# ScalarE's queue in place of SyncE's for the loads of q, k and v in an attention and mixture-of-experts kernel

## The chip, the cores and the metric

The kernel runs on one core of a Trainium2 chip. The metric is the time of one execution in device microseconds. Before the change it is 1074.55 us, the median of 3 runs (1073.31 to 1079.6).

## The reference

There are two parts, one after the other. The first is attention over 8 batches of 8 heads, 576 positions and a head size of 64, in which scores more than tau below the row's maximum are thrown away:

```python
scores = scale * np.matmul(q, k.transpose(0, 1, 3, 2))
thresh = np.max(scores, axis=-1, keepdims=True) - tau
scores = np.where(scores >= thresh, scores, -1000000000.0)
attn = np.exp(scores - np.max(scores, axis=-1, keepdims=True))
attn = attn / (np.sum(attn, axis=-1, keepdims=True) + 1e-09)
return np.matmul(attn, v)
```

The second part takes the 4608 rows of 512 numbers that come out, sends each row to one of 8 experts (the largest of 8 gate logits), computes `relu(x @ w1[e]) @ w2[e]` with 1024 hidden units and multiplies by the gate's probability.

## The kernel before

Each float32 operand is kept as a float16 pair, a high part and a low part (the rest), and a product is made of three float16 matmuls. The names end in `h`/`l` or `hi`/`lo` for these parts.

Attention goes by pairs of heads: 32 pairs, numbered n, one head in the lower 64 partitions and one in the upper. The program is written as one long list of steps, 11 per pair. A step k does one unit of scores (`s_unit`, for the row's maximum, TensorE L294 and L296, VectorE L306) of a pair that lies 21 steps ahead, one unit of transposed scores (`st_unit`, TensorE L342 and L343) of the present pair, the exponential of it on ScalarE (L359), the mask on VectorE (L362), the split of the result into two float16 parts (ScalarE's cast L367, GpSimd's subtraction L368), and a piece of the product with v (`av_piece`, L400 to L409). Beside these, functions are planned to certain steps with `plan` and `after`.

What a pair needs beforehand is done in three planned functions:

- `load_qk(n)` (L191) brings q and k of a pair, 128 partitions of 1152 float32, 576 KB, into the tile `qkf`. There are two such buffers, so the load of pair n has to wait until VectorE has made the low part of pair n-2. It is planned 15 steps ahead of `stack(n)`.
- `split(n)` (L201) makes the high part on ScalarE (L212, `hi<-qkf`, which waits for the load), and the low part in three pieces on TensorE (L226) and VectorE (L227).
- `stack(n)` (L229) copies both parts, by 12 small DMAs on SyncE's queue and one of constants, to where the matmuls read them (`QK`, `ck`, `CQ`). Later `rows` (L328) adds three rows of thresholds to `CQ` (L330).

`load_v(g)` (L196) brings v of two pairs, 640 KB, into `vf`, of which there is one buffer; `split_v` (L254) splits it with two instructions on ScalarE (L258, `vop<-vf`) and four on VectorE (L227).

When a batch is finished, its rows are normalized, written in the order of the experts to a table in device memory (`xs`), transposed by DMA on SyncE's queue (L469) and routed. The experts' matmuls (L792, L819) fill the time from about 690 us on; their weights `wf` are loaded on SyncE's queue (L697) from 512 KB pieces.

All DMAs but the indirect ones (GpSimd) are issued by SyncE. A scheduler takes the list of steps and sorts each engine's instructions by a model of its own, so that an instruction can stand earlier or later in its engine's queue than it was written; the queue of an engine then runs strictly in that order. DMAs of SyncE and ScalarE take turns in eight completion semaphores, and a DMA also waits until the one eight places before it has landed.

Of the kernel before, what the change touches and what calls it, by code (L numbers as in the profile page):

```python
# [50 lines left out]
def kernel(  # L51
# [9 lines left out]
    nc = tc.nc  # L61
# [128 lines left out]

    def load_qk(n):  # L191
        qkf = ld.tile([P, 2, S], F32, tag="qkf", name=f"qkf_{n}")
        nc.sync.dma_start(qkf, qk[n])
        st[n] = dict(qkf=qkf, Ph={}, Pl={})

    def load_v(g):  # L196
        vf = op.tile([P, 2, 10, D], F32, tag="vf", name=f"vf_{g}", bufs=1)
        nc.sync.dma_start(vf, v[g])
        gr[g] = dict(vf=vf)

    def split(n, lag=1):  # L201
# [666 lines left out]
    for n in range(NPAIR):  # L868

        k = NSTEP * (n - 1) - LEAD - SL  # L870
        if n >= 2:
            plan(max(first, k - LL), lambda n=n: load_qk(n))
        if n:
            plan(max(first, k - TUNE["sp0"]), lambda n=n: split(n))
            plan(max(first + 2, k), lambda n=n: stack(n))
    for g in range(NG):
        k = 2 * NSTEP * g
        plan(k + TUNE["sv0"], lambda g=g: split_v(g, 0))
        plan(k + TUNE["sv1"], lambda g=g: split_v(g, 1))
        if g:  # L880
            plan(k + TUNE["lv"], lambda g=g: load_v(g))
# [146 lines left out]

    if True:
        load_qk(0)  # L1030
        load_qk(1)
        load_v(0)
        split(0, 0)
        stack(0)
# [4 lines left out]
        while busy:  # L1039
# [3 lines left out]
            for z in (("st", "s"), ("s", "st"))[TUNE["ord"]]:  # L1043
                n, t = divmod(k + (NSTEP + LEAD if z == "s" else 0), NSTEP)
# [11 lines left out]
            n, t = divmod(k - TUNE["av"], NSTEP)  # L1056
# [94 lines left out]
```

## Time and profile before

| | |
|---|---|
| time, median of 3 runs | 1074.55 us (1073.31 to 1079.6) |
| time of the profiled execution | 1082.59 us |
| its span, from the first to the last instruction | 1080.9 us |
| granted TensorE clock, mean | 0.963 |
| loads of q and k, of v | 32 of 576 KB, 16 of 640 KB |

The profiled execution is one of the slower ones, 0.7% over the median. The profile gives for each engine the time in which it worked; DMA issues and waits are not counted as work. A transfer runs beside all engines, so what it costs can only be seen where an engine stands idle before the instruction that reads it. The rows of the section on the trace are from this execution.

### The profile page before, as it was taken

How to read it: one execution, taken by the hardware profiler on the slowest of the kernel's cores; microseconds unless marked ns; L12 is line 12 of the kernel's file. 1: busy time of each engine (PE TensorE's matmuls, PEld its weight loads, DVE VectorE, ACT ScalarE, POOL GpSimd, SP SyncE). 2: the span in 40 equal slices, each digit the busy share in tenths (PEclk: the TensorE clock that was granted, in tenths of full speed). 3: DMA queues.
4: the chain of work that ended last, by engine and by line, in shares of the span. 5: the costliest groups of instructions: out<-in, count | busy, mean ns of one | idle time of the engine just before them, and what ended most of it. 6: DMA issues, size and time to landing. Idle time of an engine off the chain costs nothing.

```text
span 1080.9 us, 27283 instructions
## 1 busy us (share of the span) xinstructions
PE 967.8 (90%) x10856; PEld 622.8 (58%) x10856; DVE 725.9 (67%) x1443; ACT 651.0 (60%) x1066; POOL 560.4 (52%) x460
## 2 busy tenths in 40 slices
PE   4889999799898998898897689678999999999996
PEld 1355555455555565464564366556767667766783
DVE  7888999788887989897899966451623324324550
ACT  2588887887878877787777664322433423424641
POOL 3265967876786957968667674134221222211221
PEclk9999999999999999998997789899999999999999
DMA  6435554654464643735634339869946557557620
GB/s 191 129 81 128 126 131 110 142 117 123 124 153 122 129 123 100 179 92 157 141 75 145 96 90 254 218 220 177 256 151 216 148 164 217 156 154 219 211 99 24
DMA packets 142557, 159.09 MB, mean 147 GB/s; under 512 B 96345, under 2 KB 112731, under 8 KB 142428
## 3 DMA queue, kind: packets, MB, share of 16 engines
q1 hardware_dynamic: 133276, 127.88, 46.2%
q0 software_dynamic: 9152, 29.45, 8.7%
q8 instruction: 86, 1.41, 0.5%
q14 instruction: 43, 0.35, 0.1%
HBM read 90.24 MB, written 19.44 MB: 101 GB/s over the span
## 4 chain that ended last, share of the span: by engine, by line
PE 56%; DMA 12%; DVE 7%; ACT 5%; POOL 5%; issue 4%; SPq 1%; POOLq 0%; DVEq 0%; ACTq 0%
PE h L792 18%; PE y L819 16%; PE st L342 4%; PE s L294 3%; PE st L343 3%; PE s L296 3%; DVE e L362 3%; POOL pl L368 2%; PE av L408 2%; ACT e L359 2%; ACT ph L367 2%; PE av L407 2%; PE av L409 2%; DVE nm L306 2%; DMA qkf<-in_qk_dram 2%
## 5 line engine op out<-in xcount | busy, mean ns | idle before, releaser
L368 POOL TENSOR_TENSOR pl<-e,ph 128x1024 f16<-128x1024 f32 x158 | 335.2, 2133 | 160.9 <-ACT ph L367 117.3
L362 DVE SCALAR_TENSOR_TENSOR e<-st,e 128x512 f32<-128x512 f32 (+1 forms) x352 | 221.4, 637 | 45.6 <-ACT e L359 42.9
L359 ACT ACTIVATE e<-st,ntau 128x512 f32<-128x512 f32 (+1 forms) x352 | 222.9, 650 | 37.6 <-PE st L343 34.7
L306 DVE TENSOR_REDUCE nm<-s 128x1 f32<-128x512 f32 x320 | 200.3, 632 | 33.4 <-PE s L296 32.4
L792 PEld LDWEIGHTS <-wb 128*128 128x128 f16 x2304 | 193.5, 100 | 30.4 <-DMA xTm<-R 8.4
L792 PE MATMUL h<-xTm,wb 128*128 128x256 f16 (+2 forms) x2112 | 199.0, 256 | 9.5 <-DMA xTm<-R 9.5
L819 PE MATMUL y<-wb,hl 128*128 128x512 f16 (+1 forms) x1056 | 201.3, 360 | 0.0
L367 ACT CAST ph<-e 128x1024 f16<-128x1024 f32 x160 | 166.3, 1041 | 14.5 <-DVE e L362 14.2
L408 PE MATMUL av<-vop,pl 128*128 128x65 f16 (+1 forms) x1280 | 163.2, 196 | 6.5 <-POOL pl L368 6.3
L294 PE MATMUL s<-QK 128*128 128x512 f16 (+3 forms) x640 | 141.7, 298 | 29.0 <-DMA QK<-lo 16.0
L407 PE MATMUL av<-vop,ph 128*128 128x64 f16 (+1 forms) x1280 | 164.1, 196 | 1.3 <-ACT ph L367 1.3
L409 PE MATMUL av<-vop,ph 128*128 128x65 f16 (+1 forms) x1280 | 163.1, 196 | 0.0
L711 DVE SCALAR_TENSOR_TENSOR wb<-wf,wb 128x1024 f16<-128x1024 f32 x96 | 129.4, 1384 | 49.8 <-ACT wb L710 48.5
L342 PE MATMUL st<-QK 128*128 128x512 f16 (+3 forms) x640 | 142.2, 299 | 17.2 <-DVE e L362 12.0
L819 PEld LDWEIGHTS <-hl 128*128 128x128 f16 (+1 forms) x1056 | 94.2, 100 | 98.5 <-issue 1.9
L343 PE MATMUL st<-CQ,ck 128*128 128x512 f16 (+3 forms) x640 | 141.0, 296 | 6.1 <-DMA CQ<-ptT 5.1
L408 PEld LDWEIGHTS <-pl 128*128 128x128 f16 (+1 forms) x1280 | 122.3, 102 | 41.7 <-POOL pl L368 17.7
L296 PE MATMUL s<-ck,CQ 128*128 128x512 f16 (+3 forms) x640 | 140.3, 294 | 0.0
L407 PEld LDWEIGHTS <-ph 128*128 128x128 f16 (+1 forms) x1280 | 123.3, 102 | 19.9 <-issue 8.0
L409 PEld LDWEIGHTS <-ph 128*128 128x128 f16 (+1 forms) x1280 | 122.3, 101 | 18.7 <-issue 8.6
L710 ACT ACTIVATE wb<-wf 128x1024 f16<-128x1024 f32 x96 | 97.5, 1050 | 41.1 <-DMA wf<-in_w_dram 23.0
L780 ACT ACTIVATE hl<-h 128x512 f16<-128x512 f32 (+1 forms) x80 | 45.6, 572 | 123.7 <-PE h L792 121.7
(189 smaller groups left out, 1151.1 us busy)
## 6 DMA issues: line engine op xcount, KB each, us to landing
wf<-in_w_dram SPq DMA_DIRECT2D x96, 512.0 KB
qkf<-in_qk_dram SPq DMA_DIRECT2D x32, 576.0 KB
vf<-in_v_dram SPq DMA_DIRECT2D x16, 640.0 KB
QK<-hi SPq DMA_DIRECT2D x64, 144.0 KB
QK<-hi SPq DMA_DIRECT2D x64, 72.0 KB
QK<-lo SPq DMA_DIRECT2D x64, 72.0 KB
ck<-lo SPq DMA_DIRECT2D x64, 72.0 KB
CQ<-hi SPq DMA_DIRECT2D x64, 64.0 KB
```

Of the source, the lines that this page charges most:

```text
L294: nc.tensor.matmul(sc[rows, oc], d["QA"][a][:, cols], d["KB"][a][:, CH[c]], start=True, stop=False)
L306: nc.vector.tensor_reduce(o, sc[:, 0:width(t)], axis=AX.X, op=ALU.max, negate=True)
L342: nc.tensor.matmul(sc[rows, oc], d["KB"][a][:, cols], d["QA"][a][:, CH[c]], start=True, stop=False)
L359: nc.scalar.activation(pf, sc, AF.Exp, bias=ntau, scale=0.125 / SS)
L362: nc.vector.scalar_tensor_tensor(pf, sc, 0.0, pf, ALU.is_ge, ALU.mult)
L367: nc.scalar.copy(h, pd)
L368: (nc.vector if (n, t) in PLV else nc.gpsimd).tensor_tensor(l, pd, h, ALU.subtract)
L407: nc.tensor.matmul(av[rows, a, 0:D], h, vop[:, tv, W:W + D], start=False, stop=False)
L408: nc.tensor.matmul(av[rows, a], l, vop[:, tv, 0:W], start=False, stop=False)
L409: nc.tensor.matmul(av[rows, a], h, vop[:, tv, 0:W], start=False, stop=a == 1 and i >= 2 and j == NT - 1)
L792: nc.tensor.matmul(o, Wt[:, c, wh, f], x, start=c == 0 and z == 0, stop=c == 3 and z == 2,)
L819: nc.tensor.matmul(o, h[:, hh], Wt[:, f, wh, c], start=f == 0 and z == 0, stop=f == 7 and z == 2)
```

## The change

The loads of pair 2 and later pairs of heads, and those of v from the second group of two pairs on, are issued by ScalarE. These are 30 of the 32 loads of q and k and 15 of the 16 of v. Everything else stays with the engine that has it.

```diff
     def load_qk(n):
         qkf = ld.tile([P, 2, S], F32, tag="qkf", name=f"qkf_{n}")
-        nc.sync.dma_start(qkf, qk[n])
+        (nc.sync if n < 2 else nc.scalar).dma_start(qkf, qk[n])
         st[n] = dict(qkf=qkf, Ph={}, Pl={})
 
     def load_v(g):
         vf = op.tile([P, 2, 10, D], F32, tag="vf", name=f"vf_{g}", bufs=1)
-        nc.sync.dma_start(vf, v[g])
+        (nc.sync if g == 0 else nc.scalar).dma_start(vf, v[g])
         gr[g] = dict(vf=vf)
```

The scheduler sorts again, so the queues differ in more than the moved lines. SyncE's queue before, at the loads for v of group 3 and for q and k of pair 9 (about 116 to 124 us in the trace before); `qkf_2057` is q and k of pair 9, `vf_1911` is v of group 3:

```order
L246 DMA ck_0_159<-lo_1728 64x576
L330 DMA CQ_162<-ptT_1734 1x9x128
L246 DMA ck_1_160<-lo_1728 64x576
L198 DMA vf_1911<-in_v_dram 128x1280
L193 DMA qkf_2057<-in_qk_dram 128x1152
L243 DMA QK_0_2181<-hi_2085 64x1152
L245 DMA QK_0_2181<-hi_2085 64x576
L251 DMA CQ_161<-hi_2085 64x512
```

And the same place of SyncE's queue now:

```order
L330 DMA CQ_162<-ptT_1734 1x9x128
L246 DMA ck_0_159<-lo_1728 64x576
L246 DMA ck_1_160<-lo_1728 64x576
L243 DMA QK_0_2181<-hi_2085 64x1152
L245 DMA QK_0_2181<-hi_2085 64x576
L251 DMA CQ_161<-hi_2085 64x512
```

The two loads are gone from between the copies of pair 7 into `ck` and those of pair 8 into `QK`, and the row of thresholds stands one place earlier. ScalarE's queue now, from the cast before the load to the split that reads it (`hi_2453<-qkf_2057`):

```order
L367 CAST ph_2_1739<-e_2_1738 128x1024
L193 DMA qkf_2057<-in_qk_dram 128x1152
L359 ACTIVATE e_8_1817<-st_8_1812,ntau 128x512
L198 DMA vf_1911<-in_v_dram 128x1280
L359 ACTIVATE e_10_1861<-st_10_1856,ntau 128x64
L417 COPY x_907<-av_0_1756 128x3x130
L359 ACTIVATE e_8_1817<-st_9_1888,ntau 128x512
L419 COPY x_907<-av_3_1872 128x130
L420 COPY xh_906<-av_3_1872 64x130
L367 CAST phc_10_1862<-e_10_1861 128x64
L359 ACTIVATE e_4_1928<-st_4_1925,ntau 128x512
L212 ACTIVATE hi_2453<-qkf_2057 128x1152
```

Nine rows stand between the load of q and k and the split that reads it. ScalarE's queue before, at the same place, from the row that follows the loads' time to the two splits (the split of v is `vop_166<-vf_1911`):

```order
L359 ACTIVATE e_4_1928<-st_4_1925,ntau 128x512
L367 CAST phc_10_1862<-e_10_1861 128x64
L359 ACTIVATE e_4_1928<-st_5_1951,ntau 128x512
L461 CAST R<-xn_0_2143 128x4x128
L367 CAST ph_8_1818<-e_8_1817 128x1024
L258 ACTIVATE vop_166<-vf_1911 128x10x64 x2
L359 ACTIVATE e_6_1978<-st_6_1975,ntau 128x512
L461 CAST R<-xn_1_2298 128x4x128
L359 ACTIVATE e_6_1978<-st_7_2001,ntau 128x512
L212 ACTIVATE hi_2453<-qkf_2057 128x1152
```

Before, the split of v stood ahead of that of q and k; now the split of q and k comes first, and that of v five rows behind it.

## Rows read from the trace of the kernel before

**Rows 1.** Busy times by stage: the window, its length, busy us of each engine (xinstructions), clock, DMA.

```profile
40.00:540.00 500.00, 457.57 (x6158) 273.17 (x6157) 425.77 (x898) 403.39 (x703) 370.60 (x237) 0.98 0.52 127
690.00:1081.00 391.00, 371.44 (x3009) 262.64 (x3006) 152.41 (x247) 146.06 (x193) 90.55 (x116) 0.98 0.60 172
```

**Rows 2.** ScalarE's groups by line and shape, 40 to 540 us: busy, mean ns, idle before, releasers.

```profile
L359 ACT ACTIVATE e<-st,ntau 128x512 f32<-128x512 f32 x270 | 179.9, 684 | 18.9 <-PE st L343 17.0 <-issue 0.3 <-POOL pl L368 0.3
L212 ACT ACTIVATE hi<-qkf 128x1152 f16<-128x1152 f32 x28 | 32.5, 1162 | 23.1 <-DMA qkf<-in_qk_dram 11.2 <-DMA QK<-hi 8.5 <-DMA CQ<-hi 2.4
L258 ACT ACTIVATE vop<-vf 128x640 f16<-128x640 f32 x28 | 20.2, 741 | 20.8 <-DMA vf<-in_v_dram 20.8
L417 ACT COPY x<-av 128x390 f32<-128x390 f32 x26 | 12.5, 481 | 11.7 <-PE av L409 10.3 <-PE av L408 1.4
L359 ACT ACTIVATE e<-st,ntau 128x64 f32<-128x64 f32 x27 | 8.4, 310 | 2.2 <-PE st L343 1.8
```

**Rows 3.** SyncE's issues in order of time: start us, length us, line, operation, transfer.

```profile
99.06 0.45 SPq L193 DMA_DIRECT2D qkf<-in_qk_dram  x1
...
116.65 0.48 SPq L246 DMA_DIRECT2D ck<-lo  x1
117.22 0.54 SPq L198 DMA_DIRECT2D vf<-in_v_dram  x1
117.81 0.44 SPq L193 DMA_DIRECT2D qkf<-in_qk_dram  x1
```

**Rows 4.** ScalarE in order of time: start us, length us, line, operation, [idle before, releaser].

```profile
99.34 0.23 ACT L367 CAST phc<-e 128x64 f16<-128x64 f32 x1
99.47 0.27 ACT L419 COPY x<-av 128x130 f32<-128x130 f32 x1
...
104.99 1.16 ACT L212 ACTIVATE hi<-qkf 128x1152 f16<-128x1152 f32 x1 [1.77 <-DMA CQ<-hi]
...
113.85 1.05 ACT L367 CAST ph<-e 128x1024 f16<-128x1024 f32 x1
...
121.41 1.37 ACT L258 ACTIVATE vop<-vf 128x640 f16<-128x640 f32 x2 [0.69 <-DMA vf<-in_v_dram]
```

**Rows 5.** VectorE in order of time, the last reads of the two loaded buffers.

```profile
113.67 0.53 DVE L227 SCALAR_TENSOR_TENSOR lo<-qkf,hi 128x384 f16<-128x384 f32 x1
...
114.73 0.47 DVE L227 SCALAR_TENSOR_TENSOR vop<-vf,hi_v 128x320 f16<-128x320 f32 x1
```

**Rows 6.** Lines of DMA issues, 40 to 540 us: count, shortest/median/longest ns, first and last.

```profile
L193 SPq DMA_DIRECT2D qkf<-in_qk_dram x27: 414/448/1222, 48.9 to 529.1; - x27
L198 SPq DMA_DIRECT2D vf<-in_v_dram x14: 389/535/587, 48.3 to 528.6; - x14
L469 SPq DMA_TRANSPOSE xTg<-R x27: 1254/1267/2237, 125.0 to 529.7; - x27
L549 POOL DMA_INDIRECT xs<-R,posi x22: 983/1007/1194, 194.0 to 505.5; - x22
```

**Rows 7.** Who waited for whom, 40 to 540 us: us in total, times, longest us.

```profile
PE av L400 <- ACT ph L367: 6.2, 6, 2.6
PE s L294 <- DVE e L362: 5.8, 6, 2.8
PE av L408 <- POOL pl L368: 4.6, 11, 0.7
PE av L401 <- POOL pl L368: 4.3, 7, 1.4
PE st L342 <- DVE e L362: 4.2, 9, 1.2
...
PE st L343 <- DMA CQ<-ptT: 1.2, 2, 0.6
...
DVE e L362 <- ACT e L359: 38.2, 45, 4.3
```

**Rows 8.** The chain that ended last, 40 to 540 us: start us, length us, what.

```profile
206.16 6.26 DMA qkf<-in_qk_dram
```

## The prediction

> **What bounds the kernel now.** I read the stages first, then ScalarE's groups in the stage that the change touches, then single loads, then what TensorE waits for. The change moves only loads of q, k and v, and all but four of its 45 loads fall between 40 and 540 us. In that stage [rows 1] the busy times are 458 us on TensorE, 426 on VectorE, 403 on ScalarE and 371 on GpSimd out of 500. Nothing is saturated: each pair of heads (18.5 us, 27 pairs in 500 us) goes round through all four. From 690 us on TensorE is busy 371 us of 391 with the experts' matmuls, no load of q, k or v is left there, and the change cannot reach it.
>
> The reader should look at what ScalarE waits for [rows 2]. It is idle 500 − 403 = 97 us in the stage, and 23.1 us of that stand before the split of q and k (L212), 20.8 before the split of v (L258), together 43.9 us, all put down to DMAs. Part of L212's is put down to QK<-hi and CQ<-hi, but those transfers read a buffer that is two pairs old, and the program's order issues them long before the new load. At 104.99 the split starts after 1.77 us of idleness "for CQ<-hi" [rows 4]; SyncE had issued that pair's load only at 99.06 [rows 3], 5.93 us earlier. So I count all 43.9 us as late loads.
>
> Why are they late? At 117.22 and 117.81 SyncE issues v and then q and k [rows 3]. VectorE had done with the buffer of q and k at 113.67 + 0.53 = 114.20, and with that of v at 114.73 + 0.47 = 115.20 [rows 5]. SyncE was not waiting for them: it was issuing small copies, the last from 116.65 to 117.13 [rows 3]. The queue's order made these loads 2.0 us and 3.6 us late.
>
> **The change part by part.** *SyncE* loses 30 issues of 0.448 us and 15 of 0.535 [rows 6], 13.4 + 8.0 = 21.5 us. What stands behind them in its queue, the copies into QK, ck and CQ and the rows of thresholds, goes out sooner. TensorE's only listed wait for such a transfer is 1.2 us in the stage [rows 7], since the copies are ten steps ahead of their use. I cost this at nothing; the cover is that lead, and if it were gone the price would be the issue time itself, 0.45 us a pair.
>
> *ScalarE's load waits* change because each load now has a fixed place in ScalarE's own order. In the fence of the new order the load of q and k stands after the cast of ph_2 (ended 113.85 + 1.05 = 114.90, [rows 4]), so it can go at about 114.9 where SyncE sent it at 117.81. Between it and its split stand nine rows: three exponentials of 0.684 us, a narrow one of 0.310 and a copy of 0.481 [rows 2], small ones of 0.27, 0.27 and 0.23 [rows 4] and the issue for v of 0.535: 4.15 us, and 4.60 with the load's own issue. From issue to the start of the waiting split the rows show 4.19 us (117.22 to 121.41), 5.93 (99.06 to 104.99) and 6.26 [rows 3, 4, 8]. At 5.0 us this split would still wait 0.4 us. I did the same sum for every load of the stage with the rows of the new order. The 27 loads of q and k have 3 to 12 rows in between, 3.8 us on average with the issue; the 14 of v have 5 to 13 rows, 5.8 us. With 5.0 us to land, the waits add up to 37 us for q and k and 1 us for v if ScalarE does nothing but work in between, and to 24 and 1 us if it also idles there for TensorE and VectorE as it does in this trace (0.6 us per load). I take 5.0, a little under the middle of the rows, and 30 us of waits. With the quickest landing (4.2 us) and those idle gaps it is 12 us, with the slowest (6.3) and no gaps 79; these are the ends. Against 43.9 us that is −14 us, between −32 and +35. So v gains nearly all of its 20.8 us, and q and k may lose some.
>
> *ScalarE's issues* are new: 27 × 0.448 + 14 × 0.535 = 19.6 us in the stage by SyncE's rows [rows 6]. The trace has no issue of this kind on a computing engine; GpSimd's indirect ones take 1.01 us [rows 6], but there the engine itself writes them. Below, an issue may cost nothing, because ScalarE's instructions overlap: a cast starts at 99.34 and lasts 0.23 us, and the copy behind it starts at 99.47 [rows 4], so the next one is prepared while one runs. I take 8 us, nearer to the lower end, since most loads follow an exponential or a cast of 0.68 to 1.04 us that can cover 0.45. The ends are 0 and 19.6.
>
> *A wait on ScalarE in place of one on SyncE.* The load now waits in ScalarE's queue for VectorE's last use of the buffer, with the exponentials behind it, and VectorE's masks behind those. In the example VectorE ends at 114.20 [rows 5] and ScalarE gets there at 114.90, so it costs nothing there; in the stage most loads have 0.3 to 2.7 us in hand by the same comparison. I cost it at nothing, 0.3 us per load at worst, 12 us.
>
> **The sum.** ScalarE: −14 + 8 = −6 us, between −32 and 35 + 20 + 12 = +67 us. How much of it reaches the end? TensorE's idle time that ends on ScalarE or on engines fed by it (DVE e, POOL pl, ACT ph) is 6.2 + 5.8 + 4.6 + 4.3 + 4.2 = 25.1 us in the five largest groups [rows 7]; VectorE's e itself waits 38.2 us for ScalarE [rows 7]. If all of the 25.1 came from the 43.9 us of load waits, a microsecond there is worth 0.57; if it is shared evenly over ScalarE's 97 us of idleness, 0.26. I take 0.45, nearer to the first, since the other idle time of ScalarE is mostly its wait for TensorE: −3 us; the ends, at 0.57, are −18 and +38. The profiled execution took 1082.59 us with a span of 1080.9, 0.7% above the median of 1074.55, and the waits would be a little smaller in a median run; I take the change off the median: **1071.5 us**. About 1% (10.7 us) is what a measurement of this kernel can tell from no change, as the runs before reach from 1073.31 to 1079.6. So my forecast is no change that can be told, chance 0.53.
>
> **Rivals.** *The loads cease to be a bound* (faster, 0.27). SyncE's order, not the memory, made the loads 2 to 3.6 us late [rows 3, 5]. If a load that does not queue behind SyncE's small copies lands in 4.2 us as the quickest row does [rows 3, 4], about 16 us of waits remain, and with issues hidden but for 2 us ScalarE gains 16 + 2 − 44 = −26 us; at 0.45 that is −12, 1062.5 us. Against it: the copies that follow still share the DMA engines, and the other two rows took 5.93 and 6.26 us [rows 3, 4, 8].
>
> *ScalarE pays for every issue* (slower, 0.20). One mechanism: an issue holds ScalarE's queue for its whole length, and longer when SyncE is issuing at that moment, which it does copy after copy around the loads [rows 3]; its transposes take 1.25 to 2.24 us [rows 6]. With 41 issues at 0.48 us, 0.2 us of meeting SyncE each, and a landing between 5.0 and 6.3 us (45 us of waits), ScalarE has 20 + 8 + 45 − 44 = +29 us; at 0.45 that is +13, 1087.5 us. It decides from the point where an issue costs ScalarE more than 14/41 = 0.34 us, since that eats the gain on the waits. Against it stands the overlap of short instructions.
> The Trainium skill (Perfetto Trace Analysis, section "DMA Instruction — HWDGE (DVE, Sync)") says that an issue first takes a lock on a descriptor generator that two sequencers share, and that its profiled length includes that wait. No row here has two such queues at work, so the trace neither bears it out nor denies it; by that rule the 8 us of meeting SyncE belong into the forecast as well, which would then stand at +2 us on ScalarE, 1075.5 us.
>
> *The loads go out no sooner* (no change, inside the 0.53). If ScalarE runs further ahead of VectorE than here, the wait for the buffer moves over with the load; the loads then land as late as now and ScalarE also stands still, 12 us at worst, about 1075 to 1080 us.
>
> **Range and chances.** The two rivals' own times are 1062.5 and 1087.5, with the ends of the sum at 1056 and 1112; I leave a tenth out at each end: 1059 to 1089. Faster by over 1%: 0.27; within 1%: 0.53; slower by over 1%: 0.20.
>
> **What would show it.** In the profile after: 45 issues under ScalarE's queue, with their length (0.45 to 0.54 us, or longer where SyncE is issuing); L258's idle time before it near 1 us in place of 20.8; L212's between 12 and 40 in place of 23.1; ScalarE's gap before the row that follows an issue near 0.2 us; the stage up to 540 us within some 10 us of its length, and nothing changed after 690 us. The forecast is wrong if exponentials show a new wait of the length of an issue, if L212 waits over 2 us per load, or if TensorE's idle time in the stage moves by more than 10 us with ScalarE's waits unchanged, which would mean that SyncE's queue mattered after all.

## The result, and the profile after

The changed kernel takes 1070.61 us (median of 16 runs, 1062.05 to 1075.88), the kernel before on the same chip 1081.14 us (16 runs, 1073.31 to 1085.65). The ratio is 0.9899, with a 95% interval of 0.9875 to 0.9922: 1.0% faster, about 10.9 us. The median of the first three runs of the kernel before, 1074.55 us, was a low one; in later comparisons it lies between 1073.65 and 1081.35 us, so only ratios to runs on the same chip are compared below. The profiled execution took 1071.58 us; that of the kernel before, 1082.59 us, lies 0.1% over the median of these 16 runs and is no slow one.

The busy times by stage, as in [rows 1] (window, length, busy us of TensorE, its weight loads, VectorE, ScalarE and GpSimd, clock, DMA share, GB/s). The second window reaches 11 us beyond the end of the new kernel:

```profile
40.00:540.00 500.00, 463.98 (x6368) 279.40 (x6368) 438.80 (x932) 413.14 (x721) 379.61 (x243) 1.00 0.53 129
690.00:1081.00 391.00, 355.87 (x2793) 248.70 (x2791) 142.62 (x217) 137.24 (x182) 85.95 (x114) 0.98 0.56 164
```

In the same 500 us ScalarE works 413.14 us where it worked 403.39, so its idle time fell from 96.6 to 86.9 us. The gain is made in the attention: the last product with v (L409) starts at 638.05 us where it started at 654.50, 16.5 us sooner. The span is only 11.0 us shorter (1080.9 to 1069.9), so about 5 us are given back in the part with the experts, which the change does not touch. TensorE works 397.5 us there in both; it waits longer for transposed rows (L792 12.5 us for transfers into `xTm` where it was 9.5, L483 8.4 for `xTg` where it was 6.8). In the profiles of e1, e3, e4 and e12 below this part takes 421.7 to 428.5 us, in that of the kernel before 426.2 and in this one 431.6, so one profile of each does not show that the change does it.

TensorE's granted clock in the stage rose from 0.98 [rows 1] to 1.00. One place in the kernel before shows how a late load can reach it. The split of pair 14 stands still for 2.59 us (the load of [rows 8]), TensorE works 2.60 of 5.80 us, and then its clock is at the lower of its two levels, 1.2 GHz, for 3.4 us (first a row of ScalarE, then two windows, columns as above):

```profile
212.45 1.16 ACT L212 ACTIVATE hi<-qkf 128x1152 f16<-128x1152 f32 x1 [2.59 <-DMA qkf<-in_qk_dram]
209.80:215.60 5.80, 2.60 (x29) 1.41 (x30) 3.11 (x7) 3.21 (x6) 5.80 (x6) 1.00 1.07 198
215.60:219.00 3.40, 3.40 (x14) 1.48 (x13) 3.30 (x8) 3.40 (x8) 3.40 (x3) 0.51 0.42 81
```

Up to the last product with v, TensorE is at the lower level for 58.0 us in the profile before, 34.1 us in this one and 133.1 us in that of e10 below. So part of what a wait costs may be paid through the clock; how much of the 10.9 us that is, no run here separates.

ScalarE's groups between 40 and 540 us, to be held against [rows 2]:

```profile
L359 ACT ACTIVATE e<-st,ntau 128x512 f32<-128x512 f32 x278 | 185.1, 685 | 24.9 <-PE st L343 19.5 <-DVE vop L227 1.5 <-DVE rk L537 1.0
L212 ACT ACTIVATE hi<-qkf 128x1152 f16<-128x1152 f32 x27 | 31.3, 1161 | 19.6 <-DMA CQ<-ptT 3.8 <-issue 3.7 <-DMA qkf<-in_qk_dram 3.5
L258 ACT ACTIVATE vop<-vf 128x640 f16<-128x640 f32 x28 | 19.8, 741 | 10.1 <-DMA vf<-in_v_dram 9.9
```

The idle time before the split of q and k is 19.6 us (23.1 before), before that of v 10.1 (20.8): 29.7 us in place of 43.9. The exponentials (L359) wait 24.9 us in place of 18.9, mostly for TensorE; that is where part of the saved time went.

The issues in ScalarE's queue between 40 and 540 us, which answer to the lines L193 and L198 of [rows 6] (duration in ns, minimum/median/maximum, first and last start):

```profile
L193 ACTq DMA_DIRECT2D qkf<-in_qk_dram x27: 334/335/367, 42.0 to 509.7; - x27
...
L198 ACTq DMA_DIRECT2D vf<-in_v_dram x14: 334/334/398, 43.4 to 511.9; - x14
```

An issue on ScalarE takes 0.334 us, less than SyncE's 0.448 and 0.535 [rows 6]. This length does not hold the wait for the buffer, which has to be read from the starts, below. The place of the loads of pair 9 and of v, for which [rows 3 to 5] show the kernel before, on ScalarE (start, length, idle before):

```profile
110.17 1.05 ACT L367 CAST ph<-e 128x1024 f16<-128x1024 f32 x1 [0.65 <-DVE e L362]
111.43 0.33 ACTq L193 DMA_DIRECT2D qkf<-in_qk_dram  x1
111.87 0.69 ACT L359 ACTIVATE e<-st,ntau 128x512 f32<-128x512 f32 x1 [0.65 <-DVE vop L227]
112.22 0.33 ACTq L198 DMA_DIRECT2D vf<-in_v_dram  x1
...
116.96 1.15 ACT L212 ACTIVATE hi<-qkf 128x1152 f16<-128x1152 f32 x1
...
120.25 1.37 ACT L258 ACTIVATE vop<-vf 128x640 f16<-128x640 f32 x2
```

Here both splits start without a wait. VectorE's last uses of the two buffers, as in [rows 5]:

```profile
110.86 0.53 DVE L227 SCALAR_TENSOR_TENSOR lo<-qkf,hi 128x384 f16<-128x384 f32 x1
111.33 0.87 DVE L227 SCALAR_TENSOR_TENSOR vop<-vf,hi_v 128x320 f16<-128x320 f32 x2
```

They end at 111.39 and 112.20, and the loads go out at 111.43 and 112.22, 0.04 and 0.02 us later; before it was 3.6 and 2.0 us. The same sum over the stage: the 27 loads of q and k go out 0.03 us (median) after VectorE's last use where it was 3.2, the 14 of v 0.18 where it was 1.8. So 29 of the 41 loads go out within 0.07 us of VectorE's last use: ScalarE's queue had come to the load and stood there until then.

This is not free for ScalarE. The cast ends at 111.22, the load goes out at 111.43 and its issue ends at 111.76, and the exponential behind it starts at 111.87, after 0.65 us of idle time, which is put down to VectorE's L227. The second issue runs wholly under an exponential (111.87 to 112.56). Over the stage 11.8 us of idle time stand before the rows that follow the 41 issues: 1.8 us before an issue begins, 3.0 while one runs, and 6.9 behind it, most of it for TensorE and VectorE. The other 11.0 of the 14.0 us of issues run under work.

Why did SyncE have copies to issue just when the buffers came free? Its queue in the kernel before, what ScalarE did meanwhile, and SyncE's waits at L330 between 40 and 540 us (us in total, times, longest):

```profile
104.93 0.58 SPq L251 DMA_DIRECT2D CQ<-hi  x1
111.55 0.79 SPq L330 DMA_DIRECT2D CQ<-ptT  x1
...
111.17 0.35 ACT L322 ACTIVATE ptT<-pst,thr 9x128 f16<-9x128 f32 x1
...
SPq L330 <- ACT e L359: 33.5, 19, 6.5
SPq L330 <- ACT ptT L322: 30.2, 12, 4.6
```

From 105.51 to 111.55 the queue stood at a row of thresholds, which ScalarE finished at 111.52; then it issued what had gathered behind it until 117.13, with the two loads last. In the stage it stands 63.7 us at this line for ScalarE. A load on SyncE's queue waits with it, though it needs nothing of it.

With the change SyncE was issuing while ScalarE did:

```profile
110.41 1.17 SPq L244 DMA_DIRECT2D QK<-lo  x2
111.66 0.76 SPq L330 DMA_DIRECT2D CQ<-ptT  x1
112.52 0.95 SPq L246 DMA_DIRECT2D ck<-lo  x1
```

44 of the 45 loads are issued while SyncE issues something, and it does not lengthen them. The row of thresholds (L330), which meets them most often, has a median of 0.764 us in the kernel before and in this one.

When a load has landed can be told from the DMA packets, since those of q and k have 4608 bytes and those of v 5120. ScalarE's loads make a queue of their own (packets, MB, share of the 16 engines):

```profile
q10 hardware_dynamic: 6480, 27.53, 8.7%
```

From issue to last packet (median, us):

| kernel | q and k | v |
|---|---|---|
| before: all on SyncE, v ahead of q and k | 5.04 | 4.23 |
| the change: all on ScalarE, v behind q and k | 3.76 | 6.55 |
| e1 below: q and k on ScalarE, v on SyncE | 3.81 | 5.00 |
| e2 below: v on ScalarE, q and k on SyncE | 5.13 | 4.01 |
| e9 below: all on ScalarE, v behind q and k | 3.85 | 6.55 |

Which goes out second lands later, and most so behind the other on ScalarE's queue.

What waits for ScalarE and for transfers between 40 and 540 us, as in [rows 7] (us in total, times, longest):

```profile
DVE e L362 <- ACT e L359: 23.7, 33, 2.6
PE st L343 <- DMA CQ<-ptT: 5.1, 4, 1.8
PE av L400 <- ACT ph L367: 4.6, 6, 1.2
PE st L342 <- DVE e L362: 4.4, 10, 0.9
PE s L294 <- DVE e L362: 3.4, 6, 1.6
...
PE av L401 <- POOL pl L368: 2.1, 4, 1.1
...
PE av L408 <- POOL pl L368: 1.9, 5, 0.7
```

VectorE waits 23.7 us for ScalarE's exponentials, 14.5 less than before, and the five groups of TensorE's waits that the prediction added up to 25.1 us are 16.4 us. One wait grew, for the rows of thresholds, from 1.2 to 5.1 us.

### The profile page after: what moved, and what is told of

Read it like the earlier page. It is cut to its first block, busy times and chain, and to the rows that moved or that the text cites. A ratio compares the mean times of both kernels' runs of the same rounds, so it can differ in the third digit from the quotient of the medians.

```text
span 1069.9 us, 27336 instructions
## 1 busy us (share of the span) xinstructions
PE 955.9 (89%) x10856; PEld 618.6 (58%) x10856; DVE 722.1 (67%) x1443; ACT 650.7 (61%) x1066; POOL 558.6 (52%) x460
## 3 DMA queue, kind: packets, MB, share of 16 engines
q8 instruction: 86, 1.41, 0.6%
## 4 chain that ended last, share of the span: by engine, by line
PE 50%; DMA 17%; DVE 11%; issue 9%; ACT 6%; POOL 5%; SPq 2%; POOLq 0%; DVEq 0%; ACTq 0%
PE h L792 14%; PE y L819 12%; PE s L294 4%; PE st L342 4%; DVE e L362 3%; PE st L343 3%; PE s L296 3%; ACT e L359 3%; PE av L408 3%; PE av L409 3%; DMA CQ<-ptT 3%; DVE nm L306 3%; PE av L407 2%; DMA out_dram<-o,gt 2%; DMA xs<-R,posi 2%
## 5 line engine op out<-in xcount | busy, mean ns | idle before, releaser
L359 ACT ACTIVATE e<-st,ntau 128x512 f32<-128x512 f32 (+1 forms) x352 | 221.8, 651 | 45.6 <-PE st L343 39.4
L792 PEld LDWEIGHTS <-wb 128*128 128x128 f16 x2304 | 193.2, 100 | 33.2 <-DMA xTm<-R 12.0
L792 PE MATMUL h<-xTm,wb 128*128 128x256 f16 (+2 forms) x2112 | 198.7, 256 | 12.9 <-DMA xTm<-R 12.5
L294 PE MATMUL s<-QK 128*128 128x512 f16 (+3 forms) x640 | 139.2, 294 | 26.7 <-DMA QK<-lo 17.9
L409 PE MATMUL av<-vop,ph 128*128 128x65 f16 (+1 forms) x1280 | 161.8, 196 | 0.0
L342 PE MATMUL st<-QK 128*128 128x512 f16 (+3 forms) x640 | 139.1, 293 | 24.8 <-DVE e L362 15.8
L711 DVE SCALAR_TENSOR_TENSOR wb<-wf,wb 128x1024 f16<-128x1024 f32 x96 | 120.0, 1283 | 53.5 <-ACT wb L710 51.6
L343 PE MATMUL st<-CQ,ck 128*128 128x512 f16 (+3 forms) x640 | 137.7, 291 | 10.4 <-DMA CQ<-ptT 10.4
L296 PE MATMUL s<-ck,CQ 128*128 128x512 f16 (+3 forms) x640 | 137.2, 290 | 0.0
L409 PEld LDWEIGHTS <-ph 128*128 128x128 f16 (+1 forms) x1280 | 121.8, 101 | 22.6 <-issue 10.6
```

The lines of the kernel that those rows point to most:

```text
L294: nc.tensor.matmul(sc[rows, oc], d["QA"][a][:, cols], d["KB"][a][:, CH[c]], start=True, stop=False)
L342: nc.tensor.matmul(sc[rows, oc], d["KB"][a][:, cols], d["QA"][a][:, CH[c]], start=True, stop=False)
L343: nc.tensor.matmul(sc[rows, oc], d["CK"][a][:, cols], d["CQ"][:, q], start=False, stop=True)
L359: nc.scalar.activation(pf, sc, AF.Exp, bias=ntau, scale=0.125 / SS)
L409: nc.tensor.matmul(av[rows, a], h, vop[:, tv, 0:W], start=False, stop=a == 1 and i >= 2 and j == NT - 1)
L792: nc.tensor.matmul(o, Wt[:, c, wh, f], x, start=c == 0 and z == 0, stop=c == 3 and z == 2,)
```

## The experiments

Three theories were held against each other at first. A: the time follows ScalarE's waits for loads. B: SyncE has 45 issues fewer, and what stands behind them goes out sooner. C: the scheduler sorted all engines anew, and its order is what gains. All ratios are to the kernel before on the same chip. "Waits" are ScalarE's idle us before the split of q and k and before that of v, between 40 and 540 us, from one profiled execution each.

| kernel | order | waits q/k + v | ratio (95%) |
|---|---|---|---|
| before | its own | 23.1 + 20.8 | 1 |
| the change | its own | 19.6 + 10.1 | 0.9899 (0.9875 to 0.9922) |
| e1: only q and k on ScalarE | its own | 22.8 + 4.7 | 0.9873 (0.9838 to 0.9907) |
| e2: only v on ScalarE | its own | 30.8 + 12.5 | 1.0001 (0.9971 to 1.0031) |
| e3: all on SyncE, spare buffers | its own | 12.5 + 0.3 | 0.9833 (0.9795 to 0.9871) |
| e4: the change and spare buffers | its own | 10.1 + 0.8 | 0.9717 (0.9679 to 0.9754) |
| e5: the change, 45 tiny issues on SyncE | its own | 19.8 + 12.6 | 0.9911 (0.9875 to 0.9947) |
| e6: the change, two issues a load | its own | 16.2 + 6.3 | 0.9889 (0.9848 to 0.9931) |
| e7: before, planned later | its own | 19.4 + 19.4 | 1.0011 (0.9976 to 1.0046) |
| e8: before, planned sooner | its own | 20.2 + 10.5 | 0.9955 (0.9923 to 0.9987) |
| e9: all on ScalarE | of before | 0.5 + 28.6 | 0.9995 (0.9961 to 1.0030) |
| e10: all on SyncE | of the change | 92.3 + 4.4 | 1.0809 (1.0746 to 1.0871) |
| e11: e3 with loads on ScalarE | of e3 | 7.4 + 0.2 | 0.9844 (0.9800 to 0.9888) |
| e12: e9 with spare buffers | of before | 0.0 + 0.1 | 0.9825 (0.9777 to 0.9872) |

**e1 and e2, one half of the change each.**

```diff
# e1
-        nc.sync.dma_start(qkf, qk[n])
+        (nc.sync if n < 2 else nc.scalar).dma_start(qkf, qk[n])
# e2
-        nc.sync.dma_start(vf, v[g])
+        (nc.sync if g == 0 else nc.scalar).dma_start(vf, v[g])
```

> Only the loads of q and k go to ScalarE; those of v stay with SyncE. Theory A (late loads: what counts is how long ScalarE stands idle before the splits of q, k and v): the change cut the idle time before L212 by 3.5 us and before L258 by 10.7, so this half is worth about a quarter of the 11 us: ratio to the kernel before 0.996 to 0.999, L258 still idle some 20 us. Theory B (SyncE's queue: what counts is that 45 issues leave it): 12.1 of the 19.6 us of issues leave, ratio about 0.993 to 0.995. Theory C (only the scheduler's new order): anything within 1% that does not follow the waits.

> Only the loads of v go to ScalarE; those of q and k stay with SyncE. Theory A (late loads): L258's idle time falls from 20.8 us to under 5, since a load of v that goes out at its place lands before its split, and the loads of q and k no longer stand behind those of v in one queue; ratio 0.991 to 0.994. Theory B (SyncE's queue): 7.5 of 19.6 us leave, ratio 0.995 to 0.997. Theory C: no relation to the waits.

Moving q and k alone gives all of the gain (0.9873), and most of the wait that goes is v's: 4.7 us in place of 20.8, though v is still issued by SyncE. It goes out no sooner after its buffer (1.70 us, 1.83 before, medians) and lands later; but in the new order its split comes 5.74 us after the issue where it came 4.71. Moving v alone takes 8.3 us from v's wait and adds 7.7 to that of q and k; nothing is gained. Both of A's ratios and both of B's were missed.

**e3 and e4, spare buffers**: three for q and k, two for v, so that a load needn't wait for the last use of the buffer; e3 with all loads on SyncE, e4 on top of the change.

```diff
-        qkf = ld.tile([P, 2, S], F32, tag="qkf", name=f"qkf_{n}")
+        qkf = ld.tile([P, 2, S], F32, tag="qkf", name=f"qkf_{n}", bufs=3)
-        vf = op.tile([P, 2, 10, D], F32, tag="vf", name=f"vf_{g}", bufs=1)
+        odd = g % 2 and g < NPAIR // 2 - 1
+        vf = (ld if odd else op).tile([P, 2, 10, D], F32, tag=f"vf{int(odd)}", name=f"vf_{g}", bufs=1)
```

> All loads stay with SyncE, but q and k have three buffers in place of two and v two in place of one, so that the loads go out earlier. Theory A (late loads): ScalarE's idle time before the two splits falls from 43.9 us to under 12, and the kernel gains at least what the change gained: ratio 0.980 to 0.990. Theory B (SyncE's queue): SyncE issues as much as before, ratio 0.997 to 1.003.

> The change, and the spare buffers as well. Theory A (late loads): idle time before the splits under 5 us, and about the time of the kernel with spare buffers on SyncE, 3 us to either side, ratio 0.980 to 0.990; the issues themselves cost ScalarE at most 0.1 us each since they run under the instruction before. Theory B (SyncE's queue): the time of the change, 0.988 to 0.992, and clearly under the kernel with spare buffers on SyncE.

e3 takes most of the waits away (12.8 us are left) without moving an issue, and gains more than the change. That speaks for A, but the scheduler has sorted anew here too; e12 settles it. e4 is 1.2% faster still than e3 at about the same waits (10.9 us), which neither A nor B expected; see e11.

**e5, as many issues on SyncE as before**: for each moved load SyncE issues a transfer of 4 bytes per partition.

```diff
         (nc.sync if n < 2 else nc.scalar).dma_start(qkf, qk[n])
+        if n >= 2:
+            nc.sync.dma_start(scratch[:, n:n + 1], w_gate[:, 0, 0:1])
```

> The change, but with every load that ScalarE issues SyncE issues a tiny transfer (128 rows of 4 bytes into a column that nobody reads), so that SyncE's queue has as many issues as before. Theory A (late loads): the loads still go out at their place on ScalarE, idle time before the splits about 30 us as after the change, ratio to the kernel before 0.986 to 0.993. Theory B (SyncE's queue: 45 issues fewer): the gain is given back, ratio 0.997 to 1.003.

The gain stays (0.9911), as A expected, but the run does not test B as it was meant to. The tiny transfers wait for nothing, and the scheduler put all of them early (columns as for the issues above):

```profile
L196 SPq DMA_DIRECT2D scratch<-in_w_gate_dram x27: 413/437/1445, 48.1 to 164.8; - x27
L203 SPq DMA_DIRECT2D scratch<-in_w_gate_dram x14: 425/432/588, 58.0 to 165.2; - x14
```

From 165.2 us on SyncE's queue is as light as with the change. What speaks against B are e9 and e11.

**e6, twice the issues**: each load in two halves.

```diff
-        (nc.sync if n < 2 else nc.scalar).dma_start(qkf, qk[n])
+        for w in range(2):
+            (nc.sync if n < 2 else nc.scalar).dma_start(qkf[:, w], qk[n][:, w])
```

> The change, with every load of q, k and v issued as two halves, 45 more issues on ScalarE. If an issue runs under the instruction before it: ScalarE's queue shows 90 issues of 0.33 us, ratio to the kernel before within 0.004 of the change's 0.990. If an issue holds ScalarE for its length: 45 x 0.33 = 15 us more on ScalarE, at 0.45 of it 7 us, ratio 0.995 to 0.999.

The issues on ScalarE are now 82 in the stage, some of them longer (columns as for the issues above):

```profile
L194 ACTq DMA_DIRECT2D qkf<-in_qk_dram x54: 334/337/868, 41.3 to 521.3; - x54
...
L200 ACTq DMA_DIRECT2D vf<-in_v_dram x28: 334/334/703, 43.6 to 516.0; - x28
```

Yet the ratio is 0.9889, as expected if an issue runs under the instruction before it. 41 more issues of 0.334 us and more, at least 13.7 us of ScalarE's queue, cost nothing that the time shows. ScalarE's idle time does show them: 31.3 us stand before the rows that follow an issue, where it was 11.8 with the change, while the waits before the splits are 7.2 us less (22.5 us). So the equal time is a sum of two sides, and not a proof that an issue is free.

**e7 and e8, another order by the plan alone**: the loads stay on SyncE and are planned 13 or 17 steps ahead (`ll`) in place of 15.

> The kernel before, all loads on SyncE, with the loads of q and k planned two steps later (13 ahead in place of 15); the scheduler puts TensorE's, VectorE's and ScalarE's instructions in another order, as much as the change does. Theory C (the order alone moves the time by 1%): ratio off by 0.005 or more with the idle time before the splits unchanged. Theory A (late loads): the time follows that idle time, some 0.25 us per us over 44; with 44 us it is 0.997 to 1.003.

> The kernel before, all loads on SyncE, with the loads of q and k planned two steps sooner (17 ahead); another order again. Theory C: off by 0.005 or more with the idle time before the splits unchanged. Theory A: the buffers still come free when VectorE is done with them, so the loads go out no sooner, idle time 40 to 48 us, ratio 0.996 to 1.004.

The plan changes the waits (38.8 and 30.7 us in all). e7 came out as A expected. e8 did not: A expected 40 to 48 us of waits, C a time that moves without them. It gains 0.45% with 13.2 us less of them, under half of what the change gains with 14.2 us less.

**e9 to e12, order and queue taken apart.** The program is built twice. The first build, with its loads where `order` says, only yields the order of each engine; the second moves the loads and is tied to that order by an edge from each instruction to the one ahead of it on its engine, so that only the moved loads find a place of their own. The two flags say whether q and k, and v, are on ScalarE; the lines are those of e9, e10 has the flags the other way round, e11 is built on e3, and e12 adds the spare buffers to the second build of e9.

```diff
+        for name, engine in order or ():
+            i = steps.get(name)
+            if i is None or i.engine != engine:
+                continue
+            if engine in last:
+                tc.add_manual_dep(i, last[engine], _mybir.DependencyInfo(_mybir.DependencyClass.NoSync, _mybir.DependencyReason.DATA), reason="order")
+            last[engine] = name
...
+    _, order = _build([False, False])
+    nc, _ = _build([True, True], order)
```

> Every instruction of every engine stands in the order of the kernel before; only the 45 loads are taken out of SyncE's queue and put into ScalarE's, between rows that keep their order. If the loads' own waits make the gain (ScalarE idle 43.9 us before its splits then, 29.7 with the change), ScalarE's idle time before the splits falls to 25 to 34 us and the ratio to the kernel before is 0.985 to 0.993. If it is the new order that the scheduler gave all engines, the ratio stays at 0.997 to 1.003 whatever the waits do.

e9, ScalarE's two groups, and one of v's waits (columns as above):

```profile
L212 ACT ACTIVATE hi<-qkf 128x1152 f16<-128x1152 f32 x28 | 32.5, 1159 | 0.5 <-DMA qkf<-in_qk_dram 0.4
L258 ACT ACTIVATE vop<-vf 128x640 f16<-128x640 f32 x27 | 19.4, 740 | 28.6 <-DMA vf<-in_v_dram 28.6
```

```profile
187.03 0.35 ACTq L193 DMA_DIRECT2D qkf<-in_qk_dram  x1
...
188.44 0.35 ACTq L198 DMA_DIRECT2D vf<-in_v_dram  x1
...
192.02 0.23 ACT L367 CAST phc<-e 128x64 f16<-128x64 f32 x1
196.50 1.37 ACT L258 ACTIVATE vop<-vf 128x640 f16<-128x640 f32 x2 [4.25 <-DMA vf<-in_v_dram]
```

The waits fell to 29.1 us as A expected, and the ratio stayed at 0.9995 as C expected: neither has it whole. What the queue did in the old order is a trade. q and k are no longer waited for, since the split of v stands ahead of theirs and stands still; v, which now goes out 1.41 us behind q and k on the same queue, lands 6.86 us after its issue and has its split 8.06 us after it, where the kernel before had 4.19 for v of group 3 (117.22 to 121.41). ScalarE's idle time is 97.4 us of 500 (96.6 before), so the 14.8 us saved came back: the exponentials of 512 columns wait 26.7 us in place of 18.9. That the issues eat the gain does not explain it: 13.2 us of idle time stand before the rows that follow them, about as much as with the change (11.8), which gains. Against B it is plain: SyncE has 45 issues fewer, in its old order, and nothing is gained. Whether v ahead of q and k on ScalarE would have gained in this order was not run. (This profiled run took 1084.83 us, 1.1% over its median, so its waits may be too large.)

> The mirror of the other: every engine has the order of the changed kernel, but the 45 loads stand in SyncE's queue. If the loads' own waits make the gain, ScalarE's idle time before the splits is back at 38 to 48 us and the ratio to the kernel before at 0.997 to 1.003. If the order makes it, the ratio is 0.985 to 0.993 as with the change.

e10, the load of pair 15: SyncE's queue, then VectorE, then ScalarE:

```profile
255.36 0.79 SPq L330 DMA_DIRECT2D CQ<-ptT  x1
...
258.28 0.47 SPq L246 DMA_DIRECT2D ck<-lo  x1
258.85 0.54 SPq L198 DMA_DIRECT2D vf<-in_v_dram  x1
259.45 0.45 SPq L193 DMA_DIRECT2D qkf<-in_qk_dram  x1
...
255.22 0.54 DVE L227 SCALAR_TENSOR_TENSOR lo<-qkf,hi 128x384 f16<-128x384 f32 x1
...
259.25 0.69 ACT L359 ACTIVATE e<-st,ntau 128x512 f32<-128x512 f32 x1 [0.30 <-PE st L343]
265.64 1.16 ACT L212 ACTIVATE hi<-qkf 128x1152 f16<-128x1152 f32 x1 [5.71 <-DMA qkf<-in_qk_dram]
```

Both theories expected 0.985 to 1.003 and both were wrong: 1.0809. VectorE has done with the buffer at 255.76, but SyncE issues five copies and v first, and sends the load at 259.45, 3.69 us late. In the order of the change ScalarE's next row is already the split, and it stands still for 5.71 us. Over the stage that is 92.3 us before this line. The loads are no later than in the kernel before (a median of 2.9 us behind their buffer, there 3.2); what is new is that their split stands right behind. The new order is one for early loads; without them it is the worst of all. Their places in SyncE's queue are those that the scheduler gave them in this run; others were not tried.

> The kernel with spare buffers and all loads on SyncE (ratio 0.9833, 12.8 us of waits before the splits), with the order of all its engines kept and the 45 loads put into ScalarE's queue. The kernel with spare buffers and loads on ScalarE, in an order of its own, had 0.9717 and 10.9 us. If those 1.2% come from what SyncE no longer has in its queue, the ratio is 0.967 to 0.976. If they come from the order, it stays at 0.979 to 0.987, since the waits have little left to give.

With the order of e3 kept and the loads moved, the ratio is 0.9844, that of e3 (0.9833) within the intervals: once loads are hardly waited for, it does not matter which engine issues them. So the 1.2% between e3 and e4 is order, not SyncE's queue; e11 and e4 have the same queues and buffers and differ in their order alone.

> Every engine keeps the order of the kernel before; the loads stand in ScalarE's queue and have spare buffers (three for q and k, two for v), so that hardly any load should be waited for: under 8 us before the splits, against 43.9 in the kernel before and 29.1 with its order and loads on ScalarE without spare buffers. If the waits for loads are what costs the time in any order, 36 us fewer of them give a ratio of 0.975 to 0.986, as with spare buffers in an order of their own (0.9833). If ScalarE's saved waits come back as other waits as long as the order of the kernel before stands, ScalarE's other idle time rises from 52.7 us to over 80 and the ratio is 0.994 to 1.003.

e12, ScalarE's groups:

```profile
L359 ACT ACTIVATE e<-st,ntau 128x512 f32<-128x512 f32 x285 | 190.9, 686 | 31.5 <-PE st L343 27.1 <-DVE vop L227 2.0 <-POOL R L462 0.3
L212 ACT ACTIVATE hi<-qkf 128x1152 f16<-128x1152 f32 x28 | 32.6, 1163 | 0.0
L258 ACT ACTIVATE vop<-vf 128x640 f16<-128x640 f32 x28 | 20.1, 741 | 0.1
```

Here every engine has the order of the kernel before, no load is waited for, and the ratio is 0.9825. This settles A for the old order: 43.8 us of waits gone are worth 1.75%, 18.8 of 1075.74 us, 0.43 us for each (0.31 to 0.55 by the interval). e9 has the same order and queues without the spare buffers, and gains nothing. The other part of what was expected, that all of it would come back, is wrong, though much does: the exponentials' wait rose from 18.9 to 31.5 us, and ScalarE's other idle time from 52.7 to 76.1.

The fastest version is e4, at 1049.98 us where the kernel before had 1081.35 on the same chip, and 0.9717 is below the change's 0.9899.

## Why the prediction came out as it did

**The bound.** That late loads bind in this stage was right, and e12 shows it. SyncE's small copies as their cause are seen in the rows: a median of 3.2 us between the free buffer and the issue of q and k before, 0.03 us with the change, 2.9 us in e10, where the loads are back behind the copies. Behind the copies stands a cause that I did not see: SyncE's queue stands still for ScalarE's thresholds and then has them all to issue at once.

**Waits for loads, −14 us.** The sum was right, 29.7 us measured for 30 forecast; its parts were not. v was to fall to 1 us and q and k to rise to 29; measured are 10.1 and 19.6. I used one landing time, 5.0 us, for both. With the change q and k land 3.76 us after their issue and v, second on ScalarE's queue, 6.55. The two errors cancel, so that the sum came out is luck.

**ScalarE's issues, +8 us.** The issues are shorter than SyncE's, 0.334 us, and most of their time runs under other work, as the cast in [rows 4] behind which the next copy begins had hinted. What they cost ScalarE lies between 4.8 us, its idle time before and during issues, and 11.8 us, all its idle time before the rows behind them. So 8 us is not refuted, and the lower end, 0, is.

**The share that reaches the end, 0.45.** This is the term that was too small, and the main reason why the forecast of −3 us was too small against −10.9. ScalarE does the same work in both kernels (651.0 and 650.7 us over the span), so what its idle time loses the span loses. In the stage it now does 413.14 us of work in 500 us; the 403.39 of before would take 488.2 us, 11.8 less, for 14.2 us of waits for loads gone. I had let over half of that come back as other waits, and 8 us for the issues besides; in all some 2 us came back, the issues included. At the end of the kernel the share is 10.9/14.2 = 0.77, with the interval 8.4 to 13.5 us of the ratio 0.6 to 0.95. In the old order e12 gives 0.43, which points to the new order as what makes a wait worth more than I took. The kinds of waits are not worth the same. A straight line through the table without e4 and e10 is ratio = 0.981 + 0.00067 × v's wait + 0.00025 × that of q and k: 0.72 us and 0.27 us for each us at 1075 us. No kernel in it is off by more than 0.0033, and it gives the change 10.7 × 0.72 + 3.5 × 0.27 = 8.6 us, and e9, with v 7.8 us up and q and k 22.6 us down, a gain of only 0.5 us. It is a line through twelve profiles of one run each, and e4, which is left out, lies 0.012 below it; so that v's wait weighs more is read, not shown, and why it should is open.

**The wait for the buffer on ScalarE, 0.** The price was nearly right, the reason was not. VectorE was to be done 0.3 to 2.7 us before ScalarE came to most loads; in 29 of 41 ScalarE's queue came first and stood until VectorE was done. It is cheap because ScalarE is mostly still at work on the row before: its idle time before issues is 1.8 us in all.

**SyncE's relief, 0.** Right: e9 and e11 take the loads out of SyncE's queue in a fixed order and gain nothing. e5 does not decide it, since its tiny issues all go out early.

**Rivals.** That ScalarE pays for each issue in full falls: it decides from 0.34 us of cost per issue, and 4.8 to 11.8 us over 41 issues are 0.12 to 0.29 each. Its mechanism is there in small: the sign that I gave, an exponential that waits for the length of an issue, is the row at 111.87, and 15 of the 41 rows behind an issue wait over 0.2 us. Of the other signs, the wait before the split of q and k lies where it was to lie (19.6 us), that before the split of v does not (10.1 us, not near 1), and TensorE's idle time in the stage fell by 6.4 us. The Trainium skill's rule of a shared descriptor generator (Perfetto Trace Analysis, section "DMA Instruction — HWDGE (DVE, Sync)") would have shown as longer issues where both queues are at work; 44 of 45 met one of SyncE's and the longest in the stage took 0.398 us. With two issues in a row one reaches 0.868 us, whose cause no run here shows. That loads cease to be a bound is what e3, e4, e11 and e12 are, not the change. That loads go out no sooner falls by their distance from VectorE's last use, 0.03 us in place of 3.2.

**What was missing.** I read the new order to count rows and took it for a side of the change without weight of its own. e9 shows that the moved queue in the old order gives nothing, e10 that the new order without the moved queue costs 8%. The gain of the change needs both: loads that go out early, and an order that fits them. As I read it, the split of v behind that of q and k is what fits, since v, now second on its queue, has time to land: its split comes 7.4 us after the issue (median) where it came 4.7, and it lands after 6.55. No run puts that alone to the test, and why e9 gains nothing with 14.8 us of waits gone is open.

**The time.** 1071.5 us was forecast and 1070.61 measured, but that is luck: it comes of the low median it started from. The change itself was forecast at −0.3% and is −1.0%, on the border between "within 1%" and the faster rival. "Nothing changed after 690 us" holds for the work; that about 5 us of the gain are missing at the end was not foreseen, and whether the change does it is not settled.

## What to carry to other kernels

Where the profile shows an engine waiting for loads, look when the buffer was free and when the load was issued, and whether the queue stood still for something else before. If the issuing queue was busy with small copies in between, a spare buffer mends it (1.7% here). Another queue gained less (1.0%; 2.8% with both), and in the old order it gained nothing until the spare buffers came with it (1.75%). Two loads moved to the same queue now follow each other, and the second lands later: move the right one (here q and k alone gained as much as both, v alone nothing), or give its reader more rows. Where a run adds work to keep a queue busy, look when that work was issued. Where a scheduler sorts the program anew after an edit, measure the edit once with the old order tied down, or its effect and the order's cannot be told apart.

## What the runs showed of the hardware

A load issued by ScalarE holds its queue for 0.334 us where SyncE's take 0.448 and 0.535, mostly while ScalarE's previous instruction still runs (11.0 of 14.0 us), and neither engine's issues grow when both are at it (L330: 0.764 us in both kernels). Of two loads in one queue the second lands later: v 6.55 us after its issue behind q and k on ScalarE, 4.01 where it is alone there (e2). The Trainium skill (DMA: Bandwidth & Descriptors, section "Issuing engines are not separate DMA queues") says that issuing on several engines saves only the time of the issue, usually little. e9 and e11 agree, since taking the issues off SyncE is worth nothing measurable here. What the change moved besides is the place in the queue: on SyncE a load of q and k goes out 3.2 us after its buffer is free, on ScalarE 0.03 us after, and in the order that counts on early loads their being late cost 8% (e10).
